# ReLU² attention and a gated FFN on one core: half-exchanges of attention values moved from VectorE copies to DMAs

## The chip, the core and the metric

The kernel runs on one core of one Trainium2 chip. The core has a matrix engine (TensorE, PE in the profile), a vector engine (VectorE, DVE), a scalar engine (ScalarE, ACT), GpSimd (POOL) and a sync engine (SP). Each takes its own queue of instructions in order, and they wait for each other through semaphores. SP, ACT and POOL can also issue DMAs, which 16 DMA engines carry out. The metric is the device time of one execution in microseconds: the median before is 408.68, with runs from 407.84 to 408.90.

## The reference

Attention without softmax feeds an FFN with a ReLU gate (batch B = 8, heads H = 12, sequence S = 448, head dimension D = 64, model 768, FFN 1536):

```
scores = q @ k^T / sqrt(D)
attn   = max(scores, 0)^2 / S
x      = (attn @ v), heads side by side          # 3584 rows of 768
gate   = max(x @ w_gate, 0)
out    = (gate * (x @ w_val)) @ w_out
```

The scale factors are taken out and applied once, in the FFN (`out_scale`) or on the values (`lam`).

## The kernel before

All matmuls are bf16 with 64 x 64 tiles of the array for the attention and the gate and value products, four of them at a time (`mm4`): two halves of the 128 partitions by two halves of the columns. A *quad* is four heads; a batch has three quads (`NQ` = 3), 0 to 2.

**Attention of one quad.** The transposed k and q of the batch lie in `T_b` (kqT in the profile). Seven score tiles (`tile_of`) each go through `relu2`: ACT writes the Relu of PSUM to a tile `r_sb` (L232), DVE squares it to `attn` (L233). `r_sb` comes from `rpool`, four buffers used in turn. Then seven value passes (`value_passes`) put the quad's values into two PSUM banks, with one half of the heads on partitions 0 to 63 and the other on 64 to 127.

**x in two forms.** The FFN's gate and value weights stand on different partition halves (gate on 0 to 63, value on 64 to 127), so each head's values are needed on both halves. For batches 0 to 5, `values` writes `x_of[b][0][qd]` (x0) with ACT and DVE (L266, L267), and `exchange` fills `x_of[b][1][qd]` (x1) with the halves swapped, by two DVE copies of 64 partitions x 896 (L261). For batches 6 and 7, `values_by_parity` writes the lower half to `even` and the upper to `odd`, scaled (L276 on ACT and L277 on DVE, two each), and two DVE copies (L278, L279) repeat each half on the other partitions.

**The FFN.** `gv_unit` is the gate and value product for 128 of the 1536 columns: 12 steps of four matmuls, six with x0 (e = 0) and six with x1 (e = 1), then a Relu on ACT (L320) and a product on DVE (L321) into `hT`. In the first unit of a batch the order is `BEGUN`: quads 0 and 1 of x0, quads 0 and 1 of x1, then quad 2 of x0 and last quad 2 of x1, two steps for each quad. In the other units all of x0 comes ahead of all of x1. Batches 6 and 7 go through `gv_pair` instead, which reads their x after the last batch's attention. `out_pair` is the product with w_out, after each two batches, with stores on SP and POOL (L409).

**The order.** Each instruction is pinned to its place in the program (`keep_in_program_order`). Loop `b` of the main program runs the FFN units of batch b - 1 step by step, and `spread` puts *events* of batch b between them: score tiles, value events, regroups and transposes, loads. `paced` sets the places of scores and values. The last value event of a batch 1 to 4 stands in the loop's last unit, at step 8 for batch 1 and step 5 else. In loop 2 the events of `paced` start at step 40. The FFN of batch 1 (loop 2) follows loop 1 at once; the same goes for batch 3 in loop 4 and batch 5 in loop 6. Between loops 2 and 3, and 4 and 5, there is an `out_pair`.

**SP's queue and the transposes.** From batch 2 on, k and q are transposed by DMA: DVE regroups half of a tensor (L180, into `kr` or `qr`) and right behind it the program has SP issue two transposing DMAs (L188), eight for a batch. `turned` places them in loops 1, 3, 4 and 5; in loop 2 the four regroups of batch 3 come in the last two units and all eight transposes at the last unit's step 10. In loop 1, `turned(2, units, (last - 3, 7), (last - 2, 7))` puts the k half-regroups at step 7 of the unit three ahead of the last and five steps on, and those of q one unit later. POOL holds (L677) until a batch's transposes have landed, and then issues the next loads of k and q. SP issues the transposes, stores of `out_pair`, and nothing else during these loops.

The value events that matter here, by the start of L267 or L277: (1, 0) 49.15, (1, 1) 57.65, (1, 2) 65.32, (2, 0) 84.09, (2, 1) 93.57, (3, 0) 139.50, (3, 1) 150.47, (4, 0) 174.73, (4, 1) 185.66, (5, 0) 231.65, (5, 1) 239.87, (6, 0) 258.50, (6, 1) 267.12, (6, 2) 275.86, (7, 0) 284.48, (7, 1) 293.59, (7, 2) 301.19. The pair is (batch, quad).

Of the kernel before, what the change touches and what calls it, by code (L numbers as in the profile page):

```python
# [10 lines left out]
BF16 = mybir.dt.bfloat16  # L11
AF = mybir.ActivationFunctionType
ALU = mybir.AluOpType
# [3 lines left out]
def kernel(  # L17
# [22 lines left out]
    nc = tc.nc  # L40

    B, H, S, D = q.shape
# [5 lines left out]
    NQ = HP // 2  # L48
# [4 lines left out]
    lam = 1.0 / (D * S)  # L53
# [5 lines left out]
    rpool = ctx.enter_context(tc.tile_pool(name="rpool", bufs=4))  # L59
# [6 lines left out]
    HALVES = [(c, slice(c * 64, c * 64 + 64)) for c in range(2)]  # L66

    def pin(ins):
        return tc.keep_in_program_order(ins)
# [181 lines left out]
    def value_passes(b, qd, ps, i0, i1):  # L251

        attn, v_sb = attn_of(b, qd), v_b[b % NB]
        for i in range(i0, i1):
            mm4([ps[:, r, :S] for r in range(2)], lambda r, c: v_sb[:, 2 * qd + c, i, :],
                lambda r, c: attn[:, 2 * i + c, :], i == 0, i == NC - 1)

    def exchange(b, qd):
        x0, x1 = (x_of[b][e][qd] for e in range(2))
        for (_, p), (_, other) in zip(HALVES, HALVES[::-1]):  # L260
            pin(nc.vector.tensor_copy(x1[p], x0[other]))  # L261

    def values(b, qd, ps):
        value_passes(b, qd, ps, 0, NC)
        x0 = x_of[b][0][qd]
        pin(nc.scalar.activation(x0[:, 0, :], ps[:, 0, :S], AF.Copy))  # L266
        pin(nc.vector.tensor_copy(x0[:, 1, :], ps[:, 1, :S]))  # L267
        exchange(b, qd)

    def values_by_parity(b, qd, ps):  # L270

        value_passes(b, qd, ps, 0, NC)
        even, odd = (x_of[b][e][qd] for e in range(2))
        lo, hi = (p for _, p in HALVES)
        for x, p in ((even, lo), (odd, hi)):
            pin(nc.scalar.activation(x[p, 0, :], ps[p, 0, :S], AF.Copy, scale=float(lam)))  # L276
            pin(nc.vector.tensor_scalar(x[p, 1, :], ps[p, 1, :S], float(lam), None, ALU.mult))  # L277
        pin(nc.vector.tensor_copy(even[hi], even[lo]))  # L278
        pin(nc.vector.tensor_copy(odd[lo], odd[hi]))  # L279
# [315 lines left out]
    def first_batch(units):  # L595
# [53 lines left out]
        passes(1, 4)  # L649
        value_passes(0, 2, both, 4, NC)  # L650
        exchange(0, 0)
        exchange(0, 1)
        pin(nc.scalar.activation(x_of[0][0][2], both[:, :, :S], AF.Copy))
        exchange(0, 2)
# [181 lines left out]
```

## Time and profile before

| | us |
|---|---|
| median of 3 runs | 408.68 |
| lowest and highest | 407.84, 408.90 |
| the profiled execution | 406.69 |
| its span in the profile | 404.9 |
| busy: PE | 393.0 |
| busy: DVE | 303.9 |
| busy: ACT | 244.3 |
| busy: POOL | 96.0 |
| DVE copies of `exchange` (L261), 36 | 14.7 |
| DVE copies of `values_by_parity` (L278, L279), 12 | 4.9 |

The span runs from the first instruction to the last; the profiled execution's time is the span and 1.8 us around it. In a timeline line, the columns are start, length, engine, line, operation, output and input, count; in brackets stands the idle time before it and what ended that. "SPq" lines are the instructions that SP issues for DMAs: how long they hold SP's queue, not how long the transfer takes. A wait is put down to the releaser that came last.

### The profile page before, as it was taken

The page shows a single profiled execution, that of the slowest core. Times are in us where ns is not written, and L with a number is a line of the kernel's source. Part 1 is how long each engine was busy: PE and PEld are TensorE (multiplying, and loading weights), DVE is VectorE, ACT ScalarE, POOL GpSimd, SP SyncE. Part 2 cuts the span into 40 slices and gives each one's busy share as a digit, 9 for nine tenths or more (in the row PEclk, how much of TensorE's full clock was granted, in tenths as well). Part 3 has the DMA queues.
Part 4 walks back from the last instruction along what each step waited for, and adds up shares of the span by engine and source line. Part 5 has one row for each costly group of instructions (what it writes and reads, how often), then busy time and mean ns, then how long its engine had stood idle before and what let it go on. Part 6 is the DMA issues. An engine that isn't in the chain of part 4 may idle for free.

```text
span 404.9 us, 16604 instructions
## 1 busy us (share of the span) xinstructions
PE 393.0 (97%) x7392; PEld 276.3 (68%) x7392; DVE 303.9 (75%) x532; ACT 244.3 (60%) x358; POOL 96.0 (24%) x164
## 2 busy tenths in 40 slices
PE   7899999999999999999999999999999999999994
PEld 3567767779776666666677677687777766777773
DVE  5985895599944786787833988988889869997651
ACT  3962984797334776877324889899873243434221
POOL 8833500610213601205244030020003120000240
PEclk9999999999999999999999999999999999999999
DMA  9999999799726993978946459561002350000154
GB/s 157 176 196 196 197 194 135 122 203 162 119 83 177 118 161 70 139 112 99 191 86 173 103 88 123 103 95 14 3 3 50 83 145 3 3 2 3 42 135 101
DMA packets 90984, 44.17 MB, mean 109 GB/s; under 512 B 55424, under 2 KB 89952, under 8 KB 90912
## 3 DMA queue, kind: packets, MB, share of 16 engines
q0 software_dynamic: 51136, 28.58, 49.5%
q1 hardware_dynamic: 39104, 13.99, 17.9%
q8 instruction: 58, 0.95, 0.9%
q10 hardware_dynamic: 672, 0.54, 0.5%
q14 instruction: 14, 0.11, 0.1%
HBM read 47.19 MB, written 11.01 MB: 144 GB/s over the span
## 4 chain that ended last, share of the span: by engine, by line
PE 79%; DVE 7%; DMA 5%; ACT 3%; issue 2%; SPq 2%; POOL 0%; DVEq 0%; ACTq 0%; POOLq 0%
PE ps L72 78%; DVE attn L233 4%; DMA kn<-in_k_dram 3%; ACT r_sb L232 3%; SPq L409 2%; DMA qn<-in_q_dram 1%; PE ps L208 1%; DMA out_dram<-attn 1%; DVE x L640 1%; DVE attn L399 0%; DVE kqT L209 0%; DVE hT L321 0%; ACT g_sb L320 0%; DVE kr L180 0%; DVE qr L180 0%
## 5 line engine op out<-in xcount | busy, mean ns | idle before, releaser
L72 PE MATMUL ps<-x,gv 64*64 64x448 bf16 x3552 | 203.5, 349 | 0.5 <-ACT r_sb L232 0.3
L72 PEld LDWEIGHTS <-gv 64*64 64x64 bf16 x4032 | 139.0, 107 | 54.8 <-issue 2.8
L232 ACT ACTIVATE r_sb<-ps 128x896 bf16<-128x896 f32 x167 | 147.9, 926 | 18.6 <-PE ps L72 15.1
L233 DVE TENSOR_TENSOR attn<-r_sb 128x896 bf16<-128x896 bf16 x167 | 102.2, 623 | 31.3 <-ACT r_sb L232 24.5
L72 PE MATMUL ps<-kqT 64*64 64x448 bf16 x672 | 67.9, 351 | 3.8 <-ACT r_sb L232 2.8
L72 PEld LDWEIGHTS <-hT 128*64 128x64 bf16 x1056 | 56.2, 110 | 20.8 <-issue 1.7
L409 POOL DMA_DIRECT2D out_dram<-attn x60 | 31.6, 531 | 154.0 <-DVE attn L399 121.2
L395 ACT ACTIVATE attn<-ps 128x384 f32<-128x384 f32 x64 | 28.9, 451 | 63.9 <-PE ps L72 63.3
L72 PE MATMUL ps<-wo,hT 128*64 128x384 bf16 (+1 forms) x720 | 53.9, 306 | 0.0
L321 DVE TENSOR_TENSOR hT<-ps,g_sb 128x448 bf16<-128x448 f32 x72 | 44.5, 619 | 9.2 <-ACT g_sb L320 8.6
L320 ACT ACTIVATE g_sb<-ps 128x448 bf16<-128x448 f32 x72 | 39.2, 546 | 18.5 <-PE ps L72 18.1
L399 DVE TENSOR_TENSOR attn<-ps,attn 128x384 f32<-128x384 f32 (+1 forms) x48 | 22.7, 503 | 33.4 <-ACT attn L395 19.4
L72 PEld LDWEIGHTS <-vn 64*64 64x64 bf16 (+1 forms) x840 | 30.9, 107 | 12.8 <-issue 2.3
L72 PEld LDWEIGHTS <-kqT 64*64 64x64 bf16 x672 | 27.0, 106 | 18.4 <-issue 8.4
L72 PE MATMUL ps<-attn,vn 64*64 64x448 bf16 x672 | 36.9, 350 | 0.1
L513 ACT ACTIVATE kqT<-ps 128x896 f32<-128x896 f32 x18 | 16.5, 918 | 25.0 <-PE ps L72 25.0
L116 POOL DMA_DIRECT2D vn<-in_v_dram x36 | 23.8, 681 | 23.0 <-DMA wo<-in_moe_w_out_dram 9.6
L677 POOL COPY flag<-kqT 128x1 bf16<-128x1 bf16 x12 | 3.1, 261 | 103.0 <-DMA kqT<-kr 75.9
L72 PE MATMUL ps<-o_ring,hT 128*64 128x384 bf16 (+1 forms) x336 | 25.8, 306 | 0.1
L517 DVE TENSOR_TENSOR kqT<-ps,kqT 128x896 f32<-128x896 f32 x18 | 19.5, 1084 | 5.9 <-PE ps L72 4.2
L266 ACT ACTIVATE x<-ps 128x448 bf16<-128x448 f32 x15 | 8.2, 544 | 14.4 <-PE ps L72 14.4
L261 DVE COPY x<-x 64x896 bf16<-64x896 bf16 x36 | 14.7, 408 | 2.0
(104 smaller groups left out, 289.4 us busy)
## 6 DMA issues: line engine op xcount, KB each, us to landing
out_dram<-attn SPq DMA_DIRECT2D x48, 96.0 KB, 2.6
out_dram<-attn POOLq DMA_DIRECT2D x46, 96.0 KB, 2.4
kn<-in_k_dram POOLq DMA_DIRECT2D x7, 384.0 KB, 5.9
qn<-in_q_dram POOLq DMA_DIRECT2D x7, 384.0 KB, 7.8
vn<-in_v_dram POOLq DMA_DIRECT2D x14, 192.0 KB, 9.1
gv<-in_moe_w_gate_dram POOLq DMA_DIRECT2D x6, 384.0 KB, 11.3
gv<-in_moe_w_val_dram POOLq DMA_DIRECT2D x6, 384.0 KB, 10.9
wo<-in_moe_w_out_dram POOLq DMA_DIRECT2D x2, 1152.0 KB, 12.3
```

The source lines that it names most:

```text
L72: pin(nc.tensor.matmul(o, lhsT=l, rhs=r, start=start, stop=stop, skip_group_check=True))
L116: pin(nc.gpsimd.dma_start(out=o, in_=i))
L232: pin(nc.scalar.activation(r, src, AF.Relu))
L233: pin(nc.vector.tensor_tensor(dst, r, r, ALU.mult))
L261: pin(nc.vector.tensor_copy(x1[p], x0[other]))
L320: pin(nc.scalar.activation(g_sb, o[0], AF.Relu, scale=float(out_scale)))
L321: pin(nc.vector.tensor_tensor(hT[:, mf, col:col + S], o[1], g_sb, ALU.mult))
L395: pin(nc.scalar.activation(out_of(t, r, c), bank(P, t), AF.Copy))
L399: pin(nc.vector.tensor_tensor(o, bank(Q, t), o, ALU.add))
L409: pin(engines[c].dma_start(out=rows[:, c0:c1, :], in_=src))
L513: pin(nc.scalar.activation(held(n, j), both(PQ[n][0]), AF.Copy))
L517: pin(nc.vector.tensor_tensor(k, both(PQ[n][1]), k, ALU.add))
```

## The change

In `exchange`, for quads below a limit, the two copies x1 <- x0 are DMAs issued by SP in place of DVE copies. The limit is 0 for batch 0 (none), 3 for batch 1 (all three quads), and 2 for batches 2 to 5 (quads 0 and 1). Quad 2 of batches 2 to 5 stays on DVE.

In `values_by_parity`, called for batches 6 and 7, all cases but (6, 0) and (7, 2) write both partition halves at once, one bank by ACT and one by DVE, to a tile `both` from the `r_sb` buffers; four DMAs on SP then copy the lower half to both halves of `even` and the upper half to both halves of `odd`.

```diff
     def exchange(b, qd):
         x0, x1 = (x_of[b][e][qd] for e in range(2))
         for (_, p), (_, other) in zip(HALVES, HALVES[::-1]):
-            pin(nc.vector.tensor_copy(x1[p], x0[other]))
+            if qd < {0: 0, 1: 3}.get(b, NQ - 1):
+                pin(nc.sync.dma_start(out=x1[p], in_=x0[other]))
+            else:
+                pin(nc.vector.tensor_copy(x1[p], x0[other]))
...
         value_passes(b, qd, ps, 0, NC)
         even, odd = (x_of[b][e][qd] for e in range(2))
+        if (b, qd) not in ((B - 2, 0), (B - 1, NQ - 1)):
+            both = rpool.tile([128, 2, S], BF16, name="r_sb")
+            pin(nc.scalar.activation(both[:, 0, :], ps[:, 0, :S], AF.Copy, scale=float(lam)))
+            pin(nc.vector.tensor_scalar(both[:, 1, :], ps[:, 1, :S], float(lam), None, ALU.mult))
+            for x, (_, p) in zip((even, odd), HALVES):
+                for _, o in HALVES:
+                    pin(nc.sync.dma_start(out=x[o], in_=both[p]))
+            return
         lo, hi = (p for _, p in HALVES)
```

## The prediction

> **What bounds the kernel now.** I read the page first, then SP's part of the timeline, then the engines around the end of batch 1, then the stages by windows.
>
> ```profile
> span 404.9 us, 16604 instructions
> ...
> PE 393.0 (97%) x7392; PEld 276.3 (68%) x7392; DVE 303.9 (75%) x532; ACT 244.3 (60%) x358; POOL 96.0 (24%) x164
> ```
>
> TensorE is the bound; work taken from DVE and ACT pays only where PE waits for them. By stage (columns: PE, PEld, DVE, ACT, POOL busy us, then clock, DMA share, GB/s):
>
> ```profile
> 45.00:66.00 21.00, 20.73 (x425) 14.84 (x420) 18.04 (x34) 17.29 (x24) 2.78 (x4) 1.00 1.48 183
> 66.00:75.50 9.50, 9.50 (x210) 7.22 (x204) 3.64 (x7) 3.49 (x6) 2.98 (x6) 1.00 0.67 74
> 223.50:262.00 38.50, 37.73 (x786) 26.61 (x782) 34.63 (x65) 34.18 (x48) 4.15 (x7) 1.00 0.64 101
> 262.00:303.30 41.30, 40.83 (x830) 30.92 (x824) 35.70 (x64) 36.41 (x53) 2.83 (x5) 1.00 0.21 32
> ```
>
> PE idles 0.27, 0, 0.77 and 0.47 us there: 1.5 us is all that relief of DVE and ACT can win. Of the 0.77, 0.6 is a wait for L277 of (6, 0), which the change leaves alone (the list of waits: PE behind DVE kn L277, 0.6).
>
> Next SP's queue, to which the new DMAs go. Its timeline around batches 1 and 2:
>
> ```profile
> 55.81 8.52 SPq L188 DMA_TRANSPOSE kqT<-kr  x4
> 64.38 7.10 SPq L188 DMA_TRANSPOSE kqT<-qr  x4
> 98.06 6.30 SPq L188 DMA_TRANSPOSE kqT<-kr  x4
> 104.45 5.22 SPq L188 DMA_TRANSPOSE kqT<-qr  x4
> ```
>
> Eight transposes hold SP from 55.81 to 71.48. Program order around them is seen on DVE, since each regroup (L180) is written just ahead of its transposes:
>
> ```profile
> 58.37 0.79 DVE L261 COPY x<-x 64x896 bf16<-64x896 bf16 x2
> 59.73 0.55 DVE L180 COPY qr<-qn 128x1536 bf16<-128x1536 bf16 x1
> ...
> 61.27 0.55 DVE L180 COPY qr<-qn 128x1536 bf16<-128x1536 bf16 x1
> ```
>
> So exchange (1, 1), at 58.37, stands between the kr and the qr transposes, and exchange (1, 2) behind all eight. Where (1, 2) is needed:
>
> ```profile
> 65.28 0.55 ACT L266 ACTIVATE x<-ps 128x448 bf16<-128x448 f32 x1 [1.87 <-PE ps L72]
> 66.04 0.54 ACT L320 ACTIVATE g_sb<-ps 128x448 bf16<-128x448 f32 x1 [0.21 <-PE ps L72]
> 66.05 0.81 DVE L261 COPY x<-x 64x896 bf16<-64x896 bf16 x2
> 68.31 0.55 ACT L320 ACTIVATE g_sb<-ps 128x448 bf16<-128x448 f32 x1 [1.73 <-PE ps L72]
> ```
>
> The L320 at 66.04 ends batch 0's last FFN unit, that at 68.31 batch 1's first: 12 steps in 2.27 us, 0.19 each. In that unit's order (BEGUN) the last two steps read x1 of quad 2, from 68.27 - 0.38 = 67.89. Today the copies are done at 66.86.
>
> **The change, part by part.**
>
> *Eleven exchanges leave DVE* (three of batch 1, two each of batches 2 to 5): 22 copies of 408 ns (group L261), 9.0 us. PE waits at few of their places: bounds 0 and -0.5 us (0.27 in batch 1; 0.77 - 0.6 in batch 5); I take -0.3, since DVE is 90% busy there.
>
> *Twenty-two DMAs of 112 KB join SP's queue* (and sixteen more, below; 4.3 MB beside the 44.17 MB that the page shows). The trace has no copy from SBUF to SBUF; the nearest rows are the 96 KB stores on the same queue:
>
> ```profile
> L409 SPq DMA_DIRECT2D out_dram<-attn x63: 466/553/2045, 117.7 to 401.6; - x63
> ...
> DMA to landing us min/median/max: 1.8/2.4/4.2
> ```
>
> I take 0.57 us of SP each (0.553 and a gap), 1.15 a pair, and 2.4 from issue to landing. SP runs in order; so exchange by exchange:
> - (1, 0) issues at 49.9, SP idle. Its 0.23 MB joins the loads; at 183 GB/s that is up to 1.25 us on the kn load of batch 2, which landed at 54.98 and starts the regroup. Bounds 0 and 1.25, taken as 0: all rings share the engines and the load keeps its share.
> - (1, 1) issues at 64.38, lands at 67.4; needed at unit step 6, 67.1. The 0.3 disappears in the next.
> - (1, 2) issues behind the qr transposes, which (1, 1) pushes by 1.15: SP is free at 71.48 + 1.15 = 72.63, the second DMA issues at 73.26, lands at 75.66. PE needs it at 67.89: **a stall of 7.8 us**. PE is in order, so every later unit is behind it, and ACT's L320 and DVE's L321 behind PE. From 62 to 80 the chain is PE alone, and no DMA wait stands on it until 211: nothing gives the time back. Bounds: with the set at batch 3's pace (11.6 us, 98.06 to 109.67, for 15.7) and the median landing, 71.5 and 3.7; with the longest landing and the late kn load, 7.8 + 1.8 + 1.25 = 10.8. I take 7.8, the pace of this very place.
> - Batch 2's qr transposes land 1.15 later, so POOL's hold (72.66) and the loads behind it (72.89) do too; batch 2's first score, step 40, comes after the stall. Nothing.
> - (2, 0), (2, 1): SP idle from 71.5 to 98; used after out_pair, over 10 us on. (3, 0), (5, 1): SP idle. (4, 0), (4, 1), (5, 0) stand behind transposes, with 10 us and more to spare.
> - (3, 1) stands behind batch 4's set, free at 157.7; lands 160.7 to 162.5 (landing 2.4 to 4.2); needed at 162.5 (L320 of the last unit at 161.21, a score tile, six steps). 0, no more than 0.1.
>
> *PE's pace after the stall.* The trace has one long idle of PE, ahead of its first matmul:
>
> ```profile
> 1.16 4.53 PE L72 MATMUL ps<-blank 128*64 128x448 bf16 x24 [1.16 <-DVE blank L87]
> ...
> 7.31 0.95 PE L72 MATMUL ps<-blank 128*64 128x448 bf16 x8
> ```
>
> Less the last one's own 0.58 and 0.35, a start takes 172 ns, then 86: half pace for 4.5 us, though the column PEclk says 1.00. After idles under 1 us the pace holds. An idle of 7 us lies between; a return at half pace costs 0 to 4.5 / 2 = 2.2. I take 2.2, the row that also follows an idle of several steps. The Trainium skill ("TensorE: Matmul & The Clock Gate", Part 1) puts the idle that halves the clock, and the activity that restores it, at about 3.4 us; by that, an estimate, the cost is 1.7 and the sum 0.5 lower. No row here shows an idle of that length inside the run.
>
> *Four value events by parity* ((6, 1), (6, 2), (7, 0), (7, 1)). Each loses one ACT instruction of 0.54 (2 x 0.538 become 0.544) and on DVE 2 x 0.62 + 2 x 0.39 - 0.62 = 1.4 us, and gains four DMAs. PE's idle of 0.47 at most comes back. But the staging tile is one of r_sb's four buffers: the fourth Relu after it must wait for the four DMAs. At (7, 0):
>
> ```profile
> 284.44 0.54 ACT L276 ACTIVATE kr<-ps 64x448 bf16<-64x448 f32 x1 [0.79 <-PE ps L72]
> 285.00 0.54 ACT L276 ACTIVATE qr<-ps 64x448 bf16<-64x448 f32 x1
> 285.56 0.92 ACT L232 ACTIVATE r_sb<-ps 128x896 bf16<-128x896 f32 x1
> ...
> 286.80 2.54 ACT L232 ACTIVATE r_sb<-ps 128x896 bf16<-128x896 f32 x3
> ```
>
> DVE ends at 285.1; the fourth DMA issues 3 x 0.6 later and lands at 289.3; the fourth Relu was at 288.4: 0.9 late. At the others, from the same rows, 0.5, 0.8 and 1.0: 3.2 in all, less 4 x 0.53 saved: ACT 1.1 worse. Bounds for PE -0.5 and +3.2; ACT is 88% busy, so about half of 1.1 reaches PE: +0.5. The x tiles themselves are read after 303 only.
>
> **Sum.** 406.69 (the profiled execution, span and surroundings) + 7.8 + 2.2 + 0.5 - 0.3 = 416.9. That execution is 1.99 below the median 408.68, so the median should be **418.9**.
>
> **Rivals.**
> - *PE comes back at full pace*, as after its short idles: 416.7. Against it, the idle is over ten times the 0.6 that is the longest wait of PE in the stages from 223 on. 0.2.
> - *The r_sb waits count in full*: +3.2 for +0.5, 421.6. For it, ACT issues back to back there; against it, PE has whole FFN steps between tiles. 0.1.
> - *Batch 2's set runs at the pace of the others*: stall 3.7, half the chance of a slow return, 413.7. For it, 1.24 us is the usual transpose; against it, loads fill the DMA engines at that place (183 GB/s). 0.09.
> - *Not slower.* One mechanism: SP gets through the set early enough. At the fastest transpose, 1.21, eight take 10.0 with gaps: SP is free at 55.81 + 10.0 + 1.15 = 66.96, and with the shortest landing, 1.8, the data is there at 69.4, a stall of 1.5, which the 1.5 of relief just cancels: 408.7. It decides once the second DMA lands before 69.4. 0.06 (0.04 faster by over 0.3%, 0.02 within it; 0.3% is about what a measurement of this kernel can tell from no change).
> - The forecast keeps 0.55; slower 0.94.
>
> **Range.** 413.0 to 423.0 takes in all but the last rival and the joint extremes.
>
> **What would show it.** The profile after should have PE waiting about 7 us for a DMA of x near 68 to 76, the two L188 groups there about 1.2 us apart with the exchange between, a few us of matmuls at half pace behind the wait, and from 262 to 303 ACT waiting on DMAs of x at L232. It is wrong if the DMAs of (1, 2) issue before 66, or PE's order puts other work ahead of x1 of quad 2.

## The result, and the profile after

The changed kernel takes 420.56 us (median of 6 runs, 418.85 to 421.63) against 407.77 us before (median of 6, 407.12 to 408.90). The ratio is 1.030, with a 95% interval from 1.027 to 1.032: 12.8 us slower. The profiled execution took 421.63, the slowest of the six, so its 14.9 us over the profiled execution before (406.69) are the upper end of what is to be explained.

The page of the changed kernel, span and busy times:

```profile
span 419.9 us, 16618 instructions
...
PE 398.2 (95%) x7392; PEld 301.5 (72%) x7392; DVE 289.4 (69%) x498; ACT 242.6 (58%) x354; POOL 95.4 (23%) x164
```

DVE has 14.5 us less to do, as the change says, and PE, with the same 7392 matmuls, was busy 5 us longer. Now SP's timeline around batches 1 and 2 (L262 is the new DMA of `exchange`):

```profile
56.26 8.64 SPq L188 DMA_TRANSPOSE kqT<-kr  x4
64.99 1.17 SPq L262 DMA_DIRECT2D x<-x  x2
66.27 6.05 SPq L188 DMA_TRANSPOSE kqT<-qr  x4
72.42 1.16 SPq L262 DMA_DIRECT2D x<-x  x2
```

Exchange (1, 1) stands between the kr and the qr transposes, exchange (1, 2) behind all eight, issued at 72.42. PE's timeline at the same place, with the wait ahead of a group in brackets:

```profile
65.76 1.90 PE L72 MATMUL ps<-x,gv 64*64 64x448 bf16 x36
69.39 2.01 PE L72 MATMUL ps<-x,gv 64*64 64x448 bf16 x16 [1.73 <-DMA x<-x]
74.66 8.67 PE L72 MATMUL ps<-x,gv 64*64 64x448 bf16 x118 [3.26 <-DMA x<-x]
```

PE waits twice, once for each exchange, and does 16 matmuls between. The same stage by windows shows the granted clock (the column behind POOL; 1.00 is PE's full clock):

```profile
66.50:80.50 14.00, 8.92 (x106) 4.77 (x99) 1.25 (x2) 1.24 (x3) 6.36 (x10) 0.63 0.89 150
```

In the stretch from 66.0 to 75.5 of the kernel before, the clock was 1.00 and PE was busy all the time. Here it is 0.63 on average; the trace's record of the granted clock has it at 0.5 from 69.8 to 80.1, so from 0.4 us behind the first wait on, ahead of the long one.

The second place is in the last loop of the attention. Timeline of the changed kernel (POOL's load of batch 7's values, ACT's Relu, and PE behind it):

```profile
278.29 2.64 POOL L116 DMA_DIRECT2D vn<-in_v_dram  x4 [0.33 <-PE ps L72]
...
281.31 0.91 ACT L232 ACTIVATE r_sb<-ps 128x896 bf16<-128x896 f32 x1
...
286.13 1.73 ACT L232 ACTIVATE r_sb<-ps 128x896 bf16<-128x896 f32 x2 [3.91 <-DMA x<-r_sb]
287.10 0.38 PE L72 MATMUL ps<-kqT 64*64 64x448 bf16 x4 [3.42 <-ACT r_sb L232]
```

The Relu that is fourth after value event (6, 1) waits 3.9 us for its buffer, PE 3.4 us for that Relu, and the clock record is at 0.5 again from 288.3 to 291.7.

How far the changed kernel's profiled execution is behind, read at the Relu on ACT that ends an FFN unit:

| unit | before | after | behind |
|---|---|---|---|
| last of batch 0 | 66.04 | 66.56 | 0.5 |
| first of batch 1 | 68.31 | 75.97 | 7.7 |
| second of batch 1 | 70.58 | 80.35 | 9.8 |
| second in loop 6 | 269.01 | 278.51 | 9.5 |
| fourth in loop 6 | 273.85 | 287.74 | 13.9 |
| fifth in loop 6 | 278.41 | 293.81 | 15.4 |
| end of the span | 404.9 | 419.9 | 15.0 |

Two places make nearly the whole loss, 9.3 us at the first and 5.5 at the second; between them, for 190 us, it stays between 9.5 and 10.2.

### The profile page after: what moved, and what is told of

It reads as the page before. It is cut to its first block, busy times and chain, and to the rows that moved or that the text cites. A ratio compares the mean times of both kernels' runs of the same rounds, so it can differ in the third digit from the quotient of the medians.

```text
span 419.9 us, 16618 instructions
## 1 busy us (share of the span) xinstructions
PE 398.2 (95%) x7392; PEld 301.5 (72%) x7392; DVE 289.4 (69%) x498; ACT 242.6 (58%) x354; POOL 95.4 (23%) x164
## 4 chain that ended last, share of the span: by engine, by line
PE 78%; DVE 8%; DMA 7%; ACT 3%; SPq 2%; issue 1%; POOL 0%; DVEq 0%; ACTq 0%
PE ps L72 76%; DVE attn L233 4%; DMA kn<-in_k_dram 3%; ACT r_sb L232 2%; DMA x<-r_sb 1%; DMA kr<-in_k_dram 1%; PE ps L208 1%; SPq L188 1%; SPq L283 1%; DVE hT L332 1%; DMA qr<-r_sb 1%; DMA x<-x 1%; DVE x L651 0%; DVE kqT L209 0%; ACT g_sb L331 0%
## 5 line engine op out<-in xcount | busy, mean ns | idle before, releaser
L72 PE MATMUL ps<-x,gv 64*64 64x448 bf16 x3552 | 208.9, 354 | 5.5 <-DMA x<-x 5.0
L72 PEld LDWEIGHTS <-gv 64*64 64x64 bf16 x4032 | 159.9, 108 | 45.8 <-issue 9.3
L72 PE MATMUL ps<-kqT 64*64 64x448 bf16 x672 | 71.0, 352 | 8.0 <-ACT r_sb L232 5.8
L72 PEld LDWEIGHTS <-kqT 64*64 64x64 bf16 x672 | 30.6, 107 | 19.5 <-issue 12.1
L72 PEld LDWEIGHTS <-vn 64*64 64x64 bf16 (+1 forms) x840 | 34.7, 108 | 10.6 <-issue 2.7
L72 PE MATMUL ps<-attn,vn 64*64 64x448 bf16 x672 | 38.7, 357 | 0.4 <-DVE attn L233 0.3
L116 POOL DMA_DIRECT2D qn<-in_q_dram x20 | 14.6, 751 | 1.1 <-POOLq L831 0.8
```

The lines of the kernel that those rows point to most:

```text
L72: pin(nc.tensor.matmul(o, lhsT=l, rhs=r, start=start, stop=stop, skip_group_check=True))
L116: pin(nc.gpsimd.dma_start(out=o, in_=i))
```

## The experiments

The theory: a DMA costs by where it stands in SP's queue and by what it holds until it has landed. The exchanges of batch 1 stand behind transposes, the staging tile holds a buffer that ACT needs, and an idle PE comes back at half pace. The rivals: the loss is spread over all 38 DMAs as traffic; the slow stretch has another cause; the second loss follows from the first. Each kernel below was measured beside the kernel before; ratios, and "over", are to the median of that.

**One part alone.** First `values_by_parity` as before:

```diff
-        if (b, qd) not in ((B - 2, 0), (B - 1, NQ - 1)):
+        if False:
```

> The eleven exchanges by DMA are kept, values_by_parity is as before. Theory (place in SP's queue): the loss at the start of batch 1's FFN stays whole, PE waits for x near 67 and again near 71, about 5 us of waits in all with 4 to 5 us of matmuls at half pace around them, and nothing else is lost: 9 to 10.5 us over the kernel before. Rival (the loss is spread, all 38 DMAs slow the loads and each other): with 16 DMAs fewer the loss shrinks in proportion, about 7 us over, and PE waits at other exchanges too.

Measured: 417.21 us against 407.98, ratio 1.022 (1.016 to 1.027), 9.2 us over. PE waits for x 0.6 and 4.9 us, near 68 and near 70 to 75, and nowhere else for a DMA of x, as its list of waits has it (us in total, times, longest):

```profile
PE ps L72 <- DMA x<-x: 5.4, 2, 4.9
```

The spread rival falls.

Then the exchanges as before:

```diff
-            if qd < {0: 0, 1: 3}.get(b, NQ - 1):
+            if qd < 0:
```

> values_by_parity with the staging tile and DMAs is kept, all exchanges are DVE copies as before. Theory (the staging tile holds one of r_sb's four buffers): the Relu that is fourth after the value event (6, 1) waits 3 to 4 us for the DMAs of x, PE waits about 3 us behind it and runs some us at half pace: 3 to 5 us over the kernel before. Rival (that wait comes from SP still being behind with the work that the exchanges pushed): without the exchanges it goes, and what is left is the relief of ACT and DVE, 0.5 us under to equal.

Measured: 412.69, ratio 1.012 (1.006 to 1.017), 4.7 us over. ACT's Relu still waits 3.0 us for the DMAs of x and PE 2.5 behind it, with no exchange on SP: it is a cause of its own.

```profile
276.79 1.73 ACT L232 ACTIVATE r_sb<-ps 128x896 bf16<-128x896 f32 x2 [2.99 <-DMA x<-r_sb]
```

The profiled execution, 410.82, is the fastest of four, and its clock stays at 1.00 here. The other three, for which there is no trace, had a mean clock of 0.993, for 0.996; a second half-clock stretch would fit that, but is not shown. The two parts add to 13.9, the change as a whole to 12.8.

**The place in SP's queue.** Everything as in the change, but exchange (1, 2) issued by ACT:

```diff
             if qd < {0: 0, 1: 3}.get(b, NQ - 1):
-                pin(nc.sync.dma_start(out=x1[p], in_=x0[other]))
+                e = nc.scalar if (b, qd) == (1, NQ - 1) else nc.sync
+                pin(e.dma_start(out=x1[p], in_=x0[other]))
```

> As the changed kernel, but the two DMAs of exchange (1, 2) are issued by ACT instead of SP. Theory (SP's order): the same bytes between the same places, issued at about 66.5, land by 69 to 71; the second wait near 71 (3.3 us) and most of the half pace behind it go, the first wait near 67 (1.7 us, exchange (1, 1)) stays: 5 to 6.5 us under the changed kernel, 6.5 to 8 over the one before. Rival (a copy from SBUF to SBUF beside transposes is slow wherever it is issued): they land after 73 and less than 2 us is won.

PE's timeline of this kernel:

```profile
69.07 1.30 PE L72 MATMUL ps<-x,gv 64*64 64x448 bf16 x16 [1.52 <-DMA x<-x]
70.70 0.53 PE L72 MATMUL ps<-x,gv 64*64 64x448 bf16 x2 [0.33 <-DMA x<-x]
72.02 8.98 PE L72 MATMUL ps<-x,gv 64*64 64x448 bf16 x126 [0.79 <-DMA x<-x]
```

The wait for (1, 2) falls from 3.26 to 1.1 (0.33 + 0.79), so most of it was SP's order, and beside transposes the two DMAs landed in 2.7 and 3.5 us. But the clock still falls: 0.76 over the same stretch from 66.5 to 80.5, with 0.5 on record from 70.80 to 77.62, so from behind the second of these three waits on. So only 416.68 was measured, 3.9 under the changed kernel's 420.56 where 5 to 6.5 were expected, and ratio 1.020 (1.015 to 1.026) to the kernel before. What was wrong in the expectation was the pace: I had thought that it needs the long wait. ACT also issued late, at 67.9 for 66.5: its queue stood still from 66.2 on, which the profile puts down to the kr transposes.

Only exchange (1, 0) by DMA, all else as before (below), and in another kernel (1, 0) and (1, 1), with `b == 1 and qd < 2` in the same place:

```diff
-            if qd < {0: 0, 1: 3}.get(b, NQ - 1):
+            if (b, qd) == (1, 0):
```

> Of all exchanges only (1, 0) goes by DMA; the rest of the kernel is as before. It has SP's queue to itself. Theory (place in SP's queue decides): nothing is lost, and what its 0.23 MB takes from the load of k is within what executions differ by: 0.3 us under to 1 us over the kernel before. Rival (the traffic beside the loads costs): DVE waits 0.9 us for kn at the regroup each time and 1 to 1.5 us are lost.

> Exchanges (1, 0) and (1, 1) by DMA; (1, 2) and all later ones by DVE, values_by_parity as before. Theory: (1, 1) stands behind the four kr transposes, issues near 64.9 and lands near 69; PE waits once, 0.6 to 1.9 us near 67, and the idle is too short to lose much pace: 1 to 3 us over the kernel before. Rival (the pace drops after a wait of this length too, as it seemed to in the run with the last exchange on ACT): 3 to 5 us over.

Measured: 408.26, ratio 1.0006 (0.9986 to 1.0026), with (1, 0); 410.64, ratio 1.007 (1.005 to 1.010), with both, 2.9 us over. In the first, DVE did wait 1.3 us for kn in the profiled execution, as the rival has it, and PE 1.4 behind it near 58. The medians are 0.5 us apart, within their interval (-0.6 to 1.1), so a cost of up to 1 us is not excluded. In the second PE waits 1.2 us for x, and its windows show a single wait of that length without loss of clock:

```profile
66.50:80.50 14.00, 12.80 (x268) 9.22 (x260) 5.86 (x11) 6.01 (x11) 5.59 (x9) 1.00 0.61 105
```

So by differences, of the 9.2 us about 0.5 are (1, 0)'s, 2.4 come with (1, 1) and 6 with (1, 2), the clock among them. In the changed kernel the split differs: there the wait for (1, 1) was 1.7 us, and the clock fell right behind it.

**The pace.** Matmuls on a blank tile where PE waits, work that the result doesn't use, once in the whole change and once in the exchange part alone:

```diff
+            events += [(0, 6, lambda: idle_matmuls(banks[:, 0, :], 8)), (0, 10, lambda: idle_matmuls(banks[:, 0, :], 17))]
             events += [(1, 1, lambda: load_v(3))]
```

> As the changed kernel, with matmuls on a blank tile put where PE waits in the first FFN unit of batch 1: 8 pairs ahead of step 6 and 17 pairs ahead of step 10, 1.5 and 3.2 us at full pace; they do no work of the result. The waits for the DMAs stay. Theory (an idle PE comes back at half pace): the matmuls after the wait start at 86 to 94 ns spacing or what full pace gives, and 2 to 2.5 us of the loss go. Rival (the slow stretch after the wait is something else, such as matmuls fed late by DMA or weights): the pace after the wait stays halved and the time is the changed kernel's or up to 0.5 us more.

> The exchange part alone with the 8 and 17 pairs of matmuls on a blank tile put where PE waits for x in the first FFN unit of batch 1. Theory (an idle PE comes back at half pace): beside the exchange part alone, which was 9.2 us over the kernel before, 2 to 2.5 us are won, so 6.5 to 7.5 us over, with matmuls at full pace behind the wait. Rival (the matmuls only fill the wait, and the slow stretch costs nothing that the wait would not): 9 us over stays.

PE's timeline of the exchange part with these matmuls, and its clock in the stage:

```profile
70.66 3.41 PE L72 MATMUL ps<-blank 128*64 128x448 bf16 x34
75.08 0.38 PE L72 MATMUL ps<-x,gv 64*64 64x448 bf16 x2 [1.02 <-DMA x<-x]
75.95 6.24 PE L72 MATMUL ps<-x,gv 64*64 64x448 bf16 x126 [0.48 <-DMA x<-x]
```

```profile
66.50:80.50 14.00, 12.50 (x204) 7.74 (x197) 2.40 (x4) 2.03 (x4) 5.70 (x10) 1.00 0.75 125
```

126 matmuls behind the wait take 6.24 us, where 118 took 8.67 in the change, and the clock is 1.00 in this stage of both kernels with the fill: the slow stretch is the idle's doing. From the end of the wait for (1, 2) to the Relu of the second unit, the change takes 5.7 us (74.66 to 80.35), the whole change with the fill 3.1 (77.09 to 80.16) and the exchange part with it 3.6 (75.08 to 78.65, a further wait of 0.5 in it). In the time of whole executions it is less plain: 415.66, ratio 1.021 (1.017 to 1.025), 7.9 us over where 6.5 to 7.5 were expected, beside 417.21, ratio 1.022, without the fill; and 419.74 beside 420.56 for the whole change, 0.8 under where 2 to 2.5 were expected. The intervals overlap, so the 2 to 2.5 us are shown by pace and clock, not by the time of an execution. The data came later there, which took a part of the gain: the DMAs of (1, 2) landed in 2.8 to 3.5 us, for 2.2 and 2.3 in the change, and in the whole change SP issued them at 73.56, for 72.42. Whether the fill does this is open.

**The staging tile.** The parity part alone, first with the staging tile in a part of kn or qn that is unused then, so that no buffer of `r_sb` is held:

```diff
-            both = rpool.tile([128, 2, S], BF16, name="r_sb")
+            n = 2 * ((b - (B - 2)) * NQ + qd - 1)
+            both = flat((kn_b, qn_b)[n // 6][0], HP, S)[:, n % 6:n % 6 + 2, :]
```

> values_by_parity by staging tile and DMAs alone (exchanges by DVE), but the staging tile lies in a part of kn or qn that nothing uses at that time, a new place for each of the four events, so that it holds no buffer of r_sb. Theory (the Relu's wait for its buffer is the whole loss of this part): ACT waits for no DMA of x, PE's waits in this stage fall back to those of the kernel before or less, and the loss of 4.7 us that the parity part showed alone goes: 0.5 us under to 1 us over the kernel before. Rival (the DMAs disturb the stage in another way, through SP's queue or the engines that load v): 3 us or more over stays.

Measured: 407.35 against 407.93, ratio 0.998 (0.996 to 1.0003). No engine waits for a DMA of x any more, though the longest landing is 6.2 us (5.3 with the tile in `r_sb`): the DMAs are as slow, but nothing needs the buffer.

Then with the tile in `r_sb`, and batch 7's load held back behind the DMAs of (6, 1) (`hold_unit` makes POOL wait for that FFN unit):

```diff
-            events += [(3, 1, lambda: (hold(7), load_v(7)))]
+            events += [(3, 1, lambda: (hold(7), hold_unit(5, 2), load_v(7)))]
```

> The parity part alone, staging tile in r_sb as in the change, and the load of batch 7's values waits for the FFN unit that ends near 272, so that it begins behind the DMAs of (6, 1) instead of beside them. Theory (the DMAs of (6, 1) land late, 5 to 6 us, because they share the DMA engines with that load): they land in 2.2 to 3 us, ACT's wait of 3 us at (6, 1) falls to 1 us or less, and 2 to 4 us of the 4.7 are won. Rival (they are late because of the transposes ahead of them on SP and its rings): the landing time stays above 4 us and less than 1 us is won.

Timelines of this kernel, POOL's load and ACT's fourth Relu:

```profile
273.89 2.64 POOL L116 DMA_DIRECT2D vn<-in_v_dram  x4 [0.30 <-issue]
...
274.88 1.73 ACT L232 ACTIVATE r_sb<-ps 128x896 bf16<-128x896 f32 x2 [1.43 <-DMA x<-r_sb]
```

The longest landing of the staging DMAs falls from 5.3 us (parity part alone) to 4.0, ACT's wait from 3.0 to 1.4, and the time is 408.30, ratio 1.0004 (0.9986 to 1.0022). Of the 4.7 us 4.3 are won, a little more than expected, though the landing and ACT's wait stay between theory and rival. That is more than the 1.6 us less of ACT's wait, and the two traces, of the fastest execution of the one kernel and the slowest of the other, don't tell where the rest went. By the times, the load was the larger part of it; whether the transposes ahead on SP (to 267.7 here) are the rest was not tried.

**What is left when both causes are gone.** Exchanges by DMA from batch 2 on, with the parity part as before, and then with the staging tile apart:

```diff
-            if qd < {0: 0, 1: 3}.get(b, NQ - 1):
+            if qd < {0: 0, 1: 0}.get(b, NQ - 1):
```

> Exchanges by DMA for quads 0 and 1 of batches 2 to 5 alone; batch 1 and values_by_parity as before. Theory (the loss of the exchange part is batch 1's alone): no wait of PE for a DMA of x, 6.4 us less of DVE work, none of it on the path but some tenths near 240: 0.5 us under to 0.3 us over the kernel before. Rival (each DMA on SP costs a little everywhere): 1 us or more over, with waits of PE in loops 4 and 6.

> Both parts with their two causes taken away: exchanges by DMA from batch 2 on, and the staging tile outside r_sb. Theory: no wait on a DMA of x is left, and what remains is the relief of ACT and DVE: 1.5 us under to equal to the kernel before. Rival (a third cause is left): 1 us or more over.

Measured: 408.88, ratio 1.0021 (1.0000 to 1.0042), and 407.44, ratio 0.9980 (0.9961 to 0.9999). In the first, no matmul waits for a DMA of x; its 0.9 us over miss the expected range by 0.6, at the edge of what these runs tell from nothing. Of the 1.9 us that its profiled execution is behind, 1.2 arise ahead of 66, where the two kernels are the same. The second is 0.5 us by medians, and 0.8 by the ratio, faster than the kernel before: all that 12.5 us of relieved DVE work (303.9 busy before, 291.4 here) bring.

The landing times in the kernel from batch 2 on, and in the one with (1, 0) alone:

```profile
DMA to landing us min/median/max: 2.2/5.4/6.6
```

```profile
DMA to landing us min/median/max: 5.2/5.9/6.7
```

## Why the prediction was right, and which terms were off

The direction, the main place and the mechanism were right: 418.9 was forecast from 413.0 to 423.0, 420.56 measured. By its steps:

- *Order on SP, issue and time of need.* Right. SP was to be free for (1, 2) at 72.63, and the data to land at 75.66; it issued at 72.42 and PE resumed at 74.66. No later exchange made PE wait, not (3, 1) either, whose spare time was down to nothing in the forecast.
- *The stall of 7.8 and the pace of 2.2.* Their sum, 10.0, met 9.3 in the profile; the split did not, so that the sum came out is in part luck. PE waited 5.0 us, and 4.3 went to matmuls at half pace and restarts. (1, 1) was to land at 67.4 and cost 0.3; its two DMAs took 4.1 and 4.3 us, and PE resumed at 69.39. The price from the 96 KB stores, 2.4 us, was too low there, with transposes in flight. So PE idled in two pieces, and the clock was down between them too.
- *The clock.* That PE comes back at half pace was right, and the kernels with the fill show it. The Trainium skill ("TensorE: Matmul & The Clock Gate", Part 1) has an idle window of about 3.4 us halve the clock. The trace agrees that a wait of 1.2 us leaves it at 1.00; but a single wait of 1.7 us, in the changed kernel, and two of 1.5 and 0.3 close together, with the exchange on ACT, were enough to bring it down. Single waits of 2.5 us (the parity part alone) and 2.4 (the whole change with the fill) left it at 1.00, so the length of a wait does not decide. Where it lies does: in every trace here the clock changes only at whole multiples of 3.41 us behind its first rise, and it fell only where PE had idled for half or more of the last such stretch of 3.41 us.

| kernel | stretch, us | PE idle in it, us | clock behind it |
|---|---|---|---|
| the change, first place | 66.42 to 69.83 | 1.72 | 0.5 |
| the change, second place | 284.87 to 288.28 | 2.27 | 0.5 |
| (1, 2) on ACT | 67.39 to 70.80 | 1.84 | 0.5 |
| (1, 0) and (1, 1) alone | 67.27 to 70.69 | 1.20 | 1.00 |
| parity part alone | 276.37 to 279.79 | 1.43 | 1.00 |
| whole change with the fill | 75.43 to 78.84 | 1.66 | 1.00 |

This is read out of the traces; no run was made to test it, and half is no sharp line: near the end of the kernel before, a stretch with 1.90 us of idle (397.93 to 401.34) left the clock at 1.00.

- *The r_sb wait, +0.5 with an upper bound of 3.2.* This is the term that was sized wrong: the part alone costs 4.7, the second place of the changed kernel 5.5. The mechanism was right (the fourth Relu waits for the staging DMAs), but the landing was again priced at 2.4, and for (6, 1) it was up to 6.2 beside the load of batch 7's values. So ACT waited 3.9 us there, where the forecast had 1.0 at most, and 3.4 of them reached PE. In the changed kernel this also halved the clock a second time, which no bound had counted. The rival "the r_sb waits count in full", 421.6, came nearer to the 420.56 than the forecast, though its +3.2 was still too small.
- *The relief, -0.3, and at most 1.5.* Right in size: 0.5 to 0.8 us in the kernel with both causes gone.
- *The load of kn, taken as 0.* DVE waited 0.9 us for it, within the bound of 1.25, and PE 1.0 behind DVE. In all seven traces with (1, 0) by DMA, PE waits 1.0 to 1.4 us near 58, in the six others 0.7 at most; in the times of (1, 0) alone it is within the noise.

The forecast was 10.2 us slower, and 12.8 were measured. That the time itself missed by only 1.7 is in part luck: the r_sb term was 4 us too low, the first place 0.7 too high, and the base 0.9 us lower than the one of the forecast (407.77 for 408.68).

The Trainium skill ("DMA: Bandwidth & Descriptors", "Issuing engines are not separate DMA queues") says that DMAs of all issuing engines run on the same 16 engines and interleave. The traces agree: the same 112 KB landed in 2.2 and 2.3 us for (1, 2) of the changed kernel, with no load in flight, and in 5.2 to 6.7 for (1, 0) alone, beside POOL's loads. For (1, 1) of the changed kernel it was 4.1 and 4.3, with transposes in flight and no load. What else is in flight, besides SP's order, is what a landing price from quiet stretches misses.

## What to carry to other kernels

Before a copy goes from a compute engine to a DMA, look up at its place what the issuing queue still has to do, what else the DMA engines carry, and who waits for the landing: the copy of 0.8 us became a transfer that issued 6 us late. A DMA that reads a rotating buffer holds that buffer until it has landed, so a stall comes on whichever engine needs a buffer next, here ACT for a later score tile. When the matmul engine is the bound, price a stall with the slow stretch behind it, and add up the waits that lie close together: here the idle share of stretches of 3.41 us told more than the longest wait.

## What had not been expected of the hardware

The granted clock fell to 0.5 behind a single wait of 1.7 us, and behind two of 1.5 and 0.3, but stayed at 1.00 behind single waits of 1.2, 2.4 and 2.5; in these traces it changes only at multiples of 3.41 us behind its first rise. A 112 KB copy inside SBUF landed in 2.1 to 2.2 us at best, in 4.1 to 4.3 with transposes in flight, and in up to 7.1 beside loads, a factor of three for the same bytes.
